# Where the sums of the second layer's weights are made, and how they are stored: a change to a fused attention and token-mixing kernel

## The chip, the cores and the metric

The kernel runs on one core of one Trainium2 chip, as one launch. The time of a run is the device time of that core in microseconds. Before the change the median of three runs is 777.65 us (777.59 to 778.68). The engines that matter here are PE (TensorE, matrix products), DVE (VectorE), ACT (ScalarE), POOL (GpSimd) and SP (SyncE); SP issues most of the DMAs, and ACT issues one kind of load beside its own work. Each of the two has one DMA queue.

## The reference

The first half is an attention over learned memory slots, for 8 batches, 8 heads, 576 positions, 64 channels and 32 slots; the second half is a mixer with a product over the positions and a two-layer product over the 512 channels with 1536 hidden ones:

```
a = exp(phi - max_s(phi)); a = a / sum_s(a)
k_m = a^T k;  v_m = a^T v                    # 32 x 64 for each batch and head
attn = softmax(q k_m^T / sqrt(64));  x = attn v_m      # heads side by side: 576 x 512
h = relu(x^T w_tok1) w_tok2                  # 576 -> 256 -> 576, over the positions
u = x + h^T
out = u + relu(u w_ch1) w_ch2                # 512 -> 1536 -> 512, over the channels
```

All of it is in float32. The kernel splits most values into a high and a low part in the format fp32r, and adds the products high by high, high by low and low by high.

## The kernel before, in words

**Work.** The rows of the mixer, 8 batches by 576 positions, are cut into 9 chunks of 512 rows. The two-layer product of a chunk is the bulk of PE's work. Attention runs beside it, in *quads* (one batch, four of its heads): while PE works on chunk *c*, quads whose rows are needed two or so chunks later go through it step by step. The lines `u`, `Ap`, `Rp`, `sp` of the profile are steps of the quads: `sp` (L766) are the scores, `S` (L773 to L797) the softmax on DVE, `nat` (L136, L137) the split of the attention's output that comes back from DRAM, `Ap` (L908) the first product of the token mixer with it, `Rp` (L927) the hidden part of that mixer, and `u` (L948) its second product.

**Three kinds of chunk.** Chunks 0 to 2 multiply plainly (`cp` L175 and `acc` L198). In chunks 3 to 6, the Quarters, the first layer is done with seven products in place of eight, from sums of quarters of the weights and of quarters of `x` (`qa` and `qb`, L336). Chunks 7 and 8 go together as the Double chunk, where the second layer is done so as well (`da`, `db` L401, `e` and `end` L456). The sums of weights are made once in the kernel, by two classes. `Sums(p)`, p from 0 to 5, makes those of the first layer in chunks 1 and 2 (words, four sums, a split into high and low, a store to DRAM, the rest stored straight from the weights). `Sums2(p)`, p from 0 to 5, does the same for the second layer, where a *pair* p is two of the twelve tiles of 128 hidden channels. Its sums are not read before the Double chunk. From chunk 3 on, PE works from *units*, 512 KB each, which ACT's queue loads back from DRAM (L592 for the first layer, L588 for the second), three units ahead (`AHEAD`).

**Rooms.** Tiles come from rings of rooms under a tag. The tag `c1` has twelve rooms of 4 KB in each partition. They hold the first layer's weights until chunk 3, and then the units (four alive), one tile `whole` and the parts of `x` (five in a chunk). The tag `wide` has five rooms of 8 KB; there are the `uh` and `ul` of the plain chunks, the residual `o`, the temporaries and parts of `x` of the Quarters, and the four sums of a `Sums` or a `Sums2`. A tile in a room waits until all that read or wrote the room's tile before it is done; the ring hands out rooms in the order of the program.

**Order.** The program is written out by a table of events: `at(h, f)` calls `f` when the chunks' main loop reaches the point *h*. A chunk has 24 points, so chunk *c* begins at 24*c*; in the Quarters four points make up one of the six pairs of hidden tiles. Every engine does its instructions in the order in which this table writes them, and so do the two DMA queues' issuers: an instruction that waits holds everything behind it on its engine. Here p = 0 and p = 1 of `Sums2` stand at points 44.5 and 49, at the end of chunk 1 and the beginning of chunk 2; p = 2 to 4 stand 1.5 points after the beginning of chunks 3 to 5, and p = 5 stands 5 points after that of chunk 6. Each has its steps at half-points: two `words` (L488, DVE), four `sum` (L505, DVE), `high` (L509, ACT) and `low` (L513, DVE) for each half, one `store` of 1 MB (L518, SP), and ten points after its start `store_rest` (L525, six DMAs of 128 KB on SP).

**Neighbours on SP's queue.** A quad's softmaxed scores go to DRAM and come back transposed: `rows<-S` (L863, four DMAs of 72 KB), and then `raw<-rows` (L870, L873), which the casts `nat` read. Behind them stand the memory's keys (`keys`, `kb`), `kv`, `q` and `phi` of later quads and the outputs (`out_dram<-o`, L219).

The functions that the change touches, and the lines that call them:

Of the kernel before, what the change touches and what calls it, by code (L numbers as in the profile page):

```python
# [10 lines left out]
F32 = mybir.dt.float32  # L11
F32R = mybir.dt.float32r
# [3 lines left out]
ALU = mybir.AluOpType  # L16
# [4 lines left out]
P = 128  # L21
# [7 lines left out]
def kernel(  # L29
# [25 lines left out]
    nc = tc.nc  # L55
# [8 lines left out]
    DM = w_ch2.shape[3] // 2  # L64
    TT = w_tok1.shape[2] // 2
    NF = 2 * w_ch2.shape[0]
# [9 lines left out]
    WIN, AHEAD = 3, 3  # L76
# [22 lines left out]
    sb = Rooms()  # L99
# [26 lines left out]
    c1 = {}  # L126
    c2h, c2l = {}, {}

    def f32(t):
        return t.bitcast(F32)  # L130
# [16 lines left out]
    def wide(dtype, name):  # L147

        return sb.tile([P, NKK, CW], dtype, tag="wide", name=name, bufs=5)


    class Chunk:
# [24 lines left out]
        def high(s, ps, f):  # L177
            h = sb.tile([P, CW], F32R, tag="hh", name=f"hh{f}" + s.n, bufs=2)
            l = sb.tile([P, CW], F32R, tag="hl", name=f"hl{f}" + s.n, bufs=2)
            s.hid[f] = (h, l)  # L180
            relu_high(h, ps)

        def low(s, ps, f):
            relu_low(*s.hid[f], ps)
# [33 lines left out]
        def store(s, w=slice(0, CW), channels=slice(0, NKK), eng=nc.sync):  # L218
            eng.dma_start(out=out[s.c, :, channels, w], in_=s.o[:, channels, w])  # L219
# [248 lines left out]
    class Sums2:  # L468


        to = dram.tile([P, 7, NF // 4, 1024], F32, name="sums2", tag="sums2", bufs=1)
# [4 lines left out]
        def at(s, i, n=1):  # L476
            w = slice(s.p % 2 * 512, s.p % 2 * 512 + 512)
            return s.to[:, i : i + n, s.p // 2, w]

        def words(s, j):  # L480
            h, l = (t[s.p][:, j] for t in (c2h, c2l))
            if not j:
                if s.p < 2:
                    s.w = [sb.tile([P, DM], F32, tag="al", name=f"v{j}{s.p}", bufs=2) for j in range(2)]
                else:
                    t = sb.tile([P, 2, DM], F32, tag="c1", name=f"v{s.p}", bufs=NF)
                    s.w = [t[:, j] for j in range(2)]
            nc.vector.tensor_tensor(out=s.w[j], in0=f32(h), in1=f32(l), op=ALU.add)  # L488

        def sum(s, o):  # L490
            if o == 1:
                t = wide(F32R, f"sums2{s.p}").rearrange("p a n -> p (a n)")
                s.t = t.rearrange("p (o y) -> p o y", o=4)
                s.v = t.rearrange("p (o x m) -> p o x m", o=4, x=2)

            def at(o):
                return f32(s.v[:, o, 1])

            (w11, w21), (w12, w22) = ((w[:, : DM // 2], w[:, DM // 2 :]) for w in s.w)
            if o == 1:  # L500
                x, y, op = w21, w22, ALU.add
            else:
                x, y = {0: (at(1), w11), 2: (w11, w21), 3: (w12, at(0))}[o]
                op = ALU.subtract
            nc.vector.tensor_tensor(out=at(o), in0=x, in1=y, op=op)  # L505

        def high(s, y):
            v = s.v[:, 2 * y : 2 * y + 2]
            nc.scalar.copy(out=v[:, :, 0], in_=f32(v[:, :, 1]))  # L509

        def low(s, y):
            v = s.v[:, 2 * y : 2 * y + 2]
            nc.vector.tensor_tensor(  # L513
                out=v[:, :, 1], in0=f32(v[:, :, 1]), in1=f32(v[:, :, 0]), op=ALU.subtract
            )

        def store(s):
            nc.sync.dma_start(out=s.at(2, 4), in_=f32(s.t))  # L518

        def store_rest(s):  # L520
            h, l = (t[s.p] for t in (c2h, c2l))
# [457 lines left out]
    class Piece:  # L979
# [9 lines left out]
        def __init__(s, *parts):  # L989
            s.parts, s.words = parts, sum(part.words for part in parts)  # L990
# [79 lines left out]

    class PartW2:
        words, loads, move = NT * HALF, 1, 1.6

        def __init__(s, hf):
# [14 lines left out]
    class PartC1:  # L1089


        words, loads, move = 2 * DM, 1, 2.75

        def __init__(s, f):
# [16 lines left out]

    class PartC2:
        words, loads, move = DM, 0.5, 1.375
        held = []

# [49 lines left out]
    def step(eng, us, fn, *after, take=(), use=(), move=0.0, port=False, other=None):  # L1165
        steps.append(Step(eng, us, fn, after, list(take), list(use), move, port, other))
        return steps[-1]
# [641 lines left out]
    def piece(tags, *parts, after=(), more=()):  # L1809
# [3 lines left out]
        raw = Room(*tags)  # L1813
        z = step(
            "SP", 0.5 * sum(part.loads for part in parts), lambda: p.load(raw), *after,
            take=[raw, *more], move=sum(part.move for part in parts),
        )
        loads.append(z)
# [31 lines left out]
    a, c = quads[0, 0], quads[0, 1]  # L1850
# [94 lines left out]
    z = second.plan_phi()  # L1945
    step("SP", 0.5, second.load_kv, take=[kv2], move=3.5)
    step("SP", 0.5, second.load_q, quads[1, 1].x_s, take=[q2], move=1.6)
    o0, y = Room(("wide", 5)), products[-4]
    for x in range(NKK):
        y = step(  # L1950
            "POOL", 1.4, lambda x=x: chunks[0].residual([x]), *a.lows, *c.lows, y,
            use=[*room0] + ([o0] if x else []), take=[] if x else [o0],
        )
# [30 lines left out]
    while starts[-1][:2] != (B - 1, 1):  # L1984
        b, Q, m, r = starts[-1]
        starts.append((b + Q, 1 - Q, r + 5, r + NF))
    for b, Q, m, r in starts:
        qd = second if b == 2 and not Q else Quad(b, Q)
        fine = b > 2
        if qd is not second:  # L1990
            at(max(m - (16 if b > 4 else 11), 2 * NF), qd.load_phi)
            if fine:
                w = 1.5 * ((b, Q) == (5, 0))
# [46 lines left out]
    for c in range(2, DOUBLE + 1):  # L2040
        h = 2 * NF * (c - 1)
# [18 lines left out]
    for c in range(DOUBLE):  # L2060
        h = 2 * NF * (c + 1)
# [13 lines left out]
    for n in range(AHEAD):  # L2075
        at(2 * NF * WIN - 4 + n, load_unit, n, k=1)
    for p in range(NF // 2):
        x, h = Sums2(p), 2 * NF * (WIN + p - 2) + (1.5 if p < 5 else 5) if p > 1 else 44.5 + 4.5 * p
        at(h + 10, x.store_rest, k=1)
        for y, (fn, *z) in enumerate(  # L2080
            ((x.words, 0), (x.words, 1), (x.sum, 1), (x.sum, 0), (x.sum, 3), (x.sum, 2),
             (x.high, 0), (x.low, 0), (x.high, 1), (x.low, 1), (x.store,))
        ):
            at(h + y / 2, fn, *z, k=1)
    double, h = Double(DOUBLE), 2 * NF * DOUBLE
    at(h - 12, double.mix, "T1", "12", "11", ALU.subtract, k=1)
    at(h - 11, double.high, "11", k=1)
# [20 lines left out]
    for g in range(NF, NF * WIN):  # L2108
        c, f = g // NF, g % NF
        high, low = chunks[c].ch1(f)  # L2110
        run(2 * g - 1, 1)
        run(2 * g - 0.5, -1, 0, 1)
        high()
        low()
        run(2 * g, 0)
        before[0].ch2(before[1])
        run(2 * g, 1)
        run(2 * g + 0.5, -1, 0, 1)
        run(2 * g + 1, -1, 0)
        before = (chunks[c], f)  # L2120
# [91 lines left out]
    for p in range(NF // 2):  # L2212
        h, n = 2 * NF * DOUBLE + 4 * p, n0 + 4 * p
        pool, tag = ((pat, "at"), (pch, "ch"))[p % 2]
# [3 lines left out]
        def bank_(x):  # L2218
            return pool.tile([P, CW], F32, tag=tag, name=f"d{x}{p}", bufs=2)
# [9 lines left out]
        a = bank_("a")  # L2229
# [37 lines left out]
    def gather(t, m, ps, store):  # L2267
        for a in range(2):
            o = oc[t].o[:, 2 * m + a]
            nc.vector.tensor_tensor(out=o, in0=ps[a], in1=o, op=ALU.add)  # L2270
        if store:
            oc[t].store(channels=slice(2 * m, 2 * m + 2))
# [4 lines left out]
    for i, name in enumerate(double.order[:-1]):  # L2277
        y = name in ("21", "T1", "22")
        for p in range(NF // 2):
            k = i * (NF // 2) + p  # L2280
# [20 lines left out]
    for x, (a, w, pool, tag, n) in enumerate(last):  # L2301
# [8 lines left out]
        o = oc[0].o[:, 2 + a, w]  # L2310
# [85 lines left out]
```

## Time and profile before

| | |
|---|---|
| median of 3 runs | 777.65 us (777.59 to 778.68) |
| the profiled execution | 775.13 us |
| its span (first to last instruction) | 773.3 us |
| TensorE's mean granted clock in it | 0.985 of full speed |
| PE busy | 748.2 us, 97% of the span |
| DVE, ACT, POOL busy | 516.7, 342.5, 105.1 us |
| HBM | 121.57 MB read, 35.91 MB written |

The profiled execution is one run under the profiler; its span lies 1.8 us below its own time, and its own time 2.5 us below the median of the runs. A row of the waits says which engine's line waited for which engine's line, with the sum of such idle times in us, their number and the longest. In a row of a timeline stand the start, the busy time, the engine, the line, the operation, the tile written and the tiles read; in brackets the time that the engine was idle before it and what ended that. A row of windows gives for a stretch of the span the busy time and the number of instructions of PE, PE's weight loads, DVE, ACT and POOL, and then the clock that was granted to PE, the busy share of the DMA engines and GB/s. For a DMA a timeline shows only its issue; the time until it has landed stands in the rows of the DMA issues.

### The profile page before, as it was taken

What the parts mean: (1) busy time and instruction counts of PE and PEld (TensorE: products, weight loads), DVE (VectorE), ACT (ScalarE), POOL (GpSimd) and SP (SyncE); (2) the same over time, 40 slices, a digit from 0 to 9 for tenths busy, and PEclk for the clock granted to TensorE, in tenths of its full rate; (3) what the DMA queues carried; (4) which work ended last, traced back from release to release, by engine and by line L of the source; (5) the groups of instructions that cost most, each with busy time, mean ns of one, the idle gap of its engine ahead of it and who ended that gap; (6) DMA issues with size and microseconds to landing.
All of it is one profiled execution on the core that took longest, in us unless ns stands there. A gap on an engine that the chain in (4) does not pass through costs nothing.

```text
span 773.3 us, 12829 instructions
## 1 busy us (share of the span) xinstructions
PE 748.2 (97%) x4883; PEld 639.9 (83%) x4883; DVE 516.7 (67%) x920; ACT 342.5 (44%) x740; POOL 105.1 (14%) x90
## 2 busy tenths in 40 slices
PE   9999999999998899998999899998999999999998
PEld 8777788787876688787898798987898998888886
DVE  4989874687577576874487647874585645544874
ACT  5897653242313333444363534544363544234530
POOL 2143343011302020111010101020010100000000
PEclk9999999999999799999999999999999999999999
DMA  8954631674816644869486875778475944666655
GB/s 345 415 199 157 223 102 29 172 227 134 286 17 218 231 133 151 263 206 316 140 250 238 243 264 155 269 211 306 140 211 183 279 140 152 220 192 201 217 167 189
DMA packets 98366, 158.34 MB, mean 205 GB/s; under 512 B 42112, under 2 KB 65536, under 8 KB 94208
## 3 DMA queue, kind: packets, MB, share of 16 engines
q1 hardware_dynamic: 77712, 91.05, 35.1%
q10 hardware_dynamic: 20592, 66.46, 27.6%
q8 instruction: 39, 0.64, 0.3%
q14 instruction: 23, 0.19, 0.1%
HBM read 121.57 MB, written 35.91 MB: 204 GB/s over the span
## 4 chain that ended last, share of the span: by engine, by line
PE 74%; DVE 10%; DMA 8%; ACT 3%; issue 2%; SPq 1%; POOL 1%; ACTq 0%; DVEq 0%; POOLq 0%
PE acc L198 24%; PE cp L175 8%; PE qa L336 8%; PE u L948 7%; PE qb L336 6%; PE e L456 4%; PE da L401 4%; DMA sums<-sums 3%; PE db L401 3%; PE Ap L908 3%; PE u L1610 2%; PE sp L766 1%; PE Rp L927 1%; DMA raww<-in_w_tok_dram 1%; DMA raw<-rows 1%
## 5 line engine op out<-in xcount | busy, mean ns | idle before, releaser
L198 PE MATMUL acc<-qhh,c 128*128 128x512 f32 x256 | 101.2, 401 | 0.0
L198 PE MATMUL acc<-hh,c 128*128 128x512 f32 x288 | 99.5, 405 | 0.0
L336 PEld LDWEIGHTS qb<-x,unit 128*128 128x128 f32 x432 | 62.6, 194 | 17.0 <-ACT whole L2144 11.0
L336 PE MATMUL qb<-x,unit 128*128 128x256 f32 x432 | 65.1, 288 | 9.7 <-ACT whole L2144 9.7
L336 PEld LDWEIGHTS qa<-xT,unit 128*128 128x128 f32 x432 | 62.2, 192 | 7.8 <-ACT whole L2144 1.3
L198 PEld LDWEIGHTS acc<-hh,c 128*128 128x128 f32 x288 | 55.9, 194 | 15.2 <-issue 3.2
L336 PE MATMUL qa<-xT,unit 128*128 128x256 f32 x432 | 63.7, 284 | 0.9 <-ACT whole L2144 0.9
L2147 DVE TENSOR_TENSOR whole<-whole 128x256 f32<-128x256 f32 x48 | 25.4, 528 | 56.4 <-ACT whole L2144 56.0
L198 PE MATMUL acc<-hl,c 128*128 128x512 f32 x144 | 58.0, 403 | 0.6 <-DVE hl L143 0.6
L839 POOL TENSOR_TENSOR a<-aT,a 64x576 fp32r<-64x576 f32 x22 | 34.0, 1544 | 180.0 <-ACT a L838 157.2
L198 PEld LDWEIGHTS acc<-qhh,c 128*128 128x128 f32 x256 | 49.0, 192 | 9.4 <-issue 3.3
L198 PE MATMUL acc<-qal,c 128*128 128x512 f32 x192 | 54.7, 394 | 0.0
L198 PE MATMUL acc<-qhl,c 128*128 128x512 f32 x128 | 51.4, 402 | 0.0
L175 PE MATMUL cp<-uh,c1h 128*128 128x512 f32 x144 | 51.4, 397 | 0.0
L175 PE MATMUL cp<-ul,c1h 128*128 128x512 f32 x144 | 50.3, 390 | 0.0
L175 PE MATMUL cp<-uh,c1l 128*128 128x512 f32 x144 | 50.3, 390 | 0.0
L143 DVE SCALAR_TENSOR_TENSOR hl<-cp,hh 128x512 fp32r<-128x512 f32 x36 | 24.7, 685 | 35.4 <-ACT hh L140 35.2
L2144 ACT COPY whole<-qa 128x256 f32<-128x256 f32 x72 | 26.7, 371 | 43.0 <-PE qa L336 40.1
L948 PE MATMUL u<-w2h,Rh 128*128 128x288 f32 x112 | 33.5, 299 | 3.3 <-ACT Rh L140 3.3
L198 PEld LDWEIGHTS acc<-qal,c 128*128 128x128 f32 x192 | 32.3, 189 | 3.0
L948 PE MATMUL u<-w2h,Rl 128*128 128x288 f32 x112 | 33.5, 299 | 0.7 <-DVE Rl L143 0.7
L140 ACT ACTIVATE hh<-cp 128x512 fp32r<-128x512 f32 x36 | 21.5, 597 | 26.8 <-PE cp L175 26.7
(286 smaller groups left out, 1702.7 us busy)
## 6 DMA issues: line engine op xcount, KB each, us to landing
unit<-sums ACTq DMA_DIRECT2D x111, 512.0 KB, 4.0
kv<-in_kv_dram SPq DMA_DIRECT2D x12, 1280.0 KB, 7.1
rawc<-in_w_ch_dram SPq DMA_DIRECT2D x12, 1024.0 KB, 10.4
q<-in_q_dram SPq DMA_DIRECT2D x16, 576.0 KB, 6.2
unit<-sums ACTq DMA_DIRECT2D x30, 256.0 KB, 3.6
sums<-sums SPq DMA_DIRECT2D x12, 512.0 KB, 5.7
sums<-sums SPq DMA_DIRECT2D x6, 1024.0 KB, 6.5
phi<-in_phi_dram SPq DMA_DIRECT2D x16, 320.0 KB, 4.2
```

The costliest lines, as they stand in the source:

```text
L140: nc.scalar.activation(out=h, in_=ps, func=AF.Relu)
L143: nc.vector.scalar_tensor_tensor(out=l, in0=ps, scalar=0.0, in1=f32(h), op0=ALU.max, op1=ALU.subtract)
L175: nc.tensor.matmul(ps, l[:, a, w], r[:, a], start=n == 0, stop=n == len(mm) - 1)
L198: nc.tensor.matmul(ps, l_[f // 2][:, f % 2, a * P : (a + 1) * P], r[:, w], start=f == start and x == 0, stop=f == end - 1 and x == 2,)
L336: nc.tensor.matmul(ps[:, :HW], l, r, start=first and n == 0, stop=n == len(mm) - 1, skip_group_check=not first,)
L401: nc.tensor.matmul(ps, l, r, start=first and n == 0, stop=n == len(mm) - 1, skip_group_check=not first,)
L456: nc.tensor.matmul(ps, weights[:, x, m], r[:, w], start=first and n == 0, stop=last and n == 2, skip_group_check=name in ("T2", "T3", "22"),)
L839: s.low_eng.tensor_tensor(out=l, in0=s.aT[own], in1=f32(h), op=ALU.subtract)
L908: nc.tensor.matmul(ps[:, :TT], a, w, start=x == 0, stop=x == len(mm) - 1)
L948: nc.tensor.matmul(ps[:, :HALF], a, r, start=x == 0, stop=x == len(mm) - 1)
L2144: nc.scalar.copy(out=to, in_=ps[:, :HW])
L2147: nc.vector.tensor_tensor(out=to, in0=x, in1=y, op=ALU.add)
```

## The change

`Sums2` gets two tiles of the tag `c1`, one for each half of its four sums, and makes everything inside them: the words in the high places, the sums in the low places, then the high parts over the words, then the low parts over the sums. Before, the words were in tiles of the tag `al` (p = 0, 1) or in one `c1` tile (p = 2 to 5), and the sums in a `wide` tile. The operations on DVE and ACT are the same in number and size. The store is cut into two of 512 KB, one for each half; the first follows three points after the pair's start, the second, with its `low`, 5.5 points after.

The pairs move: p = 0 to 3 stand 3.5 points after the beginning of chunks 3 to 6, p = 4 and p = 5 in the Double chunk, 1.5 and 9.5 points after its beginning. `store_rest` stands at point 84 + 12p, so from the middle of chunk 3 to the beginning of chunk 6.

```diff
         def words(s, m):
+            if m:
+                s.v = [
+                    sb.tile([P, 2, 2, DM // 2], F32R, tag="c1", name=f"v{y}{s.p}", bufs=NF)
+                    for y in range(2)
+                ]
+            h, l = (f32(t[s.p][:, :, m * DM // 2 : (m + 1) * DM // 2]) for t in (c2h, c2l))
+            nc.vector.tensor_tensor(out=f32(s.v[1 - m][:, :, 0]), in0=h, in1=l, op=ALU.add)
...
-        def store(s):
-            nc.sync.dma_start(out=s.at(2, 4), in_=f32(s.t))
+        def store(s, y):
+            t = s.v[y].rearrange("p o x m -> p o (x m)")
+            nc.sync.dma_start(out=s.at(2 + 2 * y, 2), in_=f32(t))
...
-        x, h = Sums2(p), 2 * NF * (WIN + p - 2) + (1.5 if p < 5 else 5) if p > 1 else 44.5 + 4.5 * p
-        at(h + 10, x.store_rest, k=1)
-        for y, (fn, *z) in enumerate(
-            ((x.words, 0), (x.words, 1), (x.sum, 1), (x.sum, 0), (x.sum, 3), (x.sum, 2),
-             (x.high, 0), (x.low, 0), (x.high, 1), (x.low, 1), (x.store,))
+        x, h = Sums2(p), 2 * NF * (WIN + min(p, 4)) + (3.5, 1.5, 9.5)[max(p - 3, 0)]
+        at(2 * NF * WIN + 12 + 12 * p, x.store_rest, k=1)
+        for y, fn, *z in (
+            (0, x.words, 1), (0.5, x.words, 0), (0.5, x.sum, 1), (1, x.sum, 0), (1, x.sum, 2),
+            (1.5, x.sum, 3), (2, x.high, 0), (2.5, x.high, 1), (3, x.low, 0), (3, x.store, 0),
+            (5.5, x.low, 1), (5.5, x.store, 1),
         ):
-            at(h + y / 2, fn, *z, k=1)
+            at(h + y, fn, *z, k=1)
```

The order on two engines shows what moves. The number at the end of a name counts tiles through the program and differs between the two kernels; line numbers above 480 are eleven smaller in the changed kernel. The first place is DVE at the end of chunk 1, from the reduction of a quad's `phi` to the softmax `S` of another quad. Before, with `v` and `sums` of pair 0 of `Sums2`:

```order
L621 TENSOR_REDUCE pr_1_2146<-phi_1_1900 128x128
L505 TENSOR_TENSOR sums_2150<-v_2128,v_2129 128x256
L143 SCALAR_TENSOR_TENSOR hl_1_2153<-cp_1_2132,hh_1_2152 128x512
L230 TENSOR_TENSOR ul_1668<-u_2_1_2156,uh_1667 128x288
L230 TENSOR_TENSOR ul_1668<-u_2_1_2167,uh_1667 128x96
L773 STREAM_TRANSPOSE S_0_2189<-sp_3_0_2179 128x288
L773 STREAM_TRANSPOSE S_0_2189<-sp_3_0_2180 128x288
L505 TENSOR_TENSOR sums_2150<-sums_2150,v_2128 128x256
L780 TENSOR_REDUCE mx_0_2205<-S_0_2189 128x18
L505 TENSOR_TENSOR sums_2150<-v_2129,sums_2150 128x256
```

The same place of the changed kernel:

```order
L610 TENSOR_REDUCE pr_1_2142<-phi_1_1900 128x128
L143 SCALAR_TENSOR_TENSOR hl_1_2147<-cp_1_2129,hh_1_2146 128x512
L230 TENSOR_TENSOR ul_1668<-u_2_1_2150,uh_1667 128x288
L230 TENSOR_TENSOR ul_1668<-u_2_1_2161,uh_1667 128x96
L762 STREAM_TRANSPOSE S_0_2183<-sp_3_0_2173 128x288
L762 STREAM_TRANSPOSE S_0_2183<-sp_3_0_2174 128x288
L769 TENSOR_REDUCE mx_0_2198<-S_0_2183 128x18
```

The sums of pair 0 no longer stand in front of `hl` and `ul`, nor between the steps of the softmax.

The second place is SP's queue in chunk 3. There `rows`, `raw`, `keys` and `kb` belong to a quad, `kv` to a later one, and `sums_101` is the DRAM tile that all of `Sums2` writes. Before:

```order
L863 DMA rows_1_3439<-S_1_3335 32x18x32 x4
L518 DMA sums_101<-sums_3245 128x4x512
L870 DMA raw_1_3492<-rows_1_3439 128x4x128
L873 DMA raw_1_3492<-rows_1_3439 64x128
L719 DMA keys_0_3500<-T_0_3497 32x2x32 x4
L612 DMA kv_1_3538<-in_kv_dram 128x2560
L728 DMA kb_0_3587<-keys_0_3500 64x128 x2
```

The same place of the changed kernel, where `v_3234` and `v_3235` are the two halves of pair 0:

```order
L852 DMA rows_1_3397<-S_1_3291 32x18x32 x4
L507 DMA sums_101<-v_3234 128x2x512
L859 DMA raw_1_3451<-rows_1_3397 128x4x128
L862 DMA raw_1_3451<-rows_1_3397 64x128
L708 DMA keys_0_3459<-T_0_3456 32x2x32 x4
L601 DMA kv_1_3497<-in_kv_dram 128x2560
L507 DMA sums_101<-v_3235 128x2x512
L717 DMA kb_0_3548<-keys_0_3459 64x128 x2
```

Between `rows` and `raw` stands half a store in place of a whole one, and the other half stands behind `kv`, in front of `kb`. Chunks 4 and 5 have the same order. In chunk 6 the store of before stood behind `raw`, and now the first half stands in front of it there as well:

```order
L863 DMA rows_1_6376<-S_1_6293 32x18x32 x4
L870 DMA raw_1_6423<-rows_1_6376 128x4x128
L873 DMA raw_1_6423<-rows_1_6376 64x128
L518 DMA sums_101<-sums_6361 128x4x512
L525 DMA sums_101<-c_1242 128x256 x6
```

The changed kernel in chunk 6:

```order
L852 DMA rows_1_6362<-S_1_6277 32x18x32 x4
L507 DMA sums_101<-v_6236 128x2x512
L859 DMA raw_1_6408<-rows_1_6362 128x4x128
L862 DMA raw_1_6408<-rows_1_6362 64x128
L507 DMA sums_101<-v_6237 128x2x512
```

The six DMAs of `store_rest` that followed there now stand in front of this piece, at the beginning of the chunk.

## Rows read from the trace of the kernel before

**Rows 1.** The page's first part: busy time of each engine.

```profile
PE 748.2 (97%) x4883; PEld 639.9 (83%) x4883; DVE 516.7 (67%) x920; ACT 342.5 (44%) x740; POOL 105.1 (14%) x90
```

**Rows 2.** Waits of PE: line, releaser, us in total, times, longest.

```profile
PE qb L336 <- ACT whole L2144: 9.7, 3, 3.5
PE u L948 <- ACT Rh L140: 3.3, 1, 3.3
PE sp L766 <- DVE ul L230: 1.7, 1, 1.7
...
PE Ap L908 <- DVE nat L137: 1.4, 2, 1.2
...
PE acc L198 <- DVE hl L143: 0.6, 1, 0.6
```

**Rows 3.** Waits of DVE, the two for a room.

```profile
DVE sums L560 <- DMA out_dram<-o: 4.9, 1, 4.9
...
DVE sums L505 <- POOL o L210: 2.4, 1, 2.4
```

**Rows 4.** Waits of ACT, the one for a DMA of `sums`.

```profile
ACT x L285 <- DMA sums<-sums: 8.8, 3, 3.4
```

**Rows 5.** Windows of 20 us: early chunks, chunk 3, chunk 6, Double chunk.

```profile
200.00:220.00 20.00, 18.30 (x100) 15.12 (x99) 11.41 (x20) 5.25 (x12) 6.98 (x5) 0.91 0.52 165
240.00:260.00 20.00, 15.54 (x76) 11.11 (x75) 13.85 (x25) 5.71 (x12) 2.26 (x2) 0.82 0.86 317
340.00:360.00 20.00, 16.61 (x96) 14.68 (x95) 13.26 (x28) 9.05 (x23) 2.85 (x2) 0.91 0.85 262
580.00:600.00 20.00, 20.00 (x140) 17.48 (x139) 12.02 (x26) 7.05 (x20) 0.00 (x0) 1.00 0.55 183
660.00:680.00 20.00, 20.00 (x90) 16.58 (x89) 9.75 (x15) 6.79 (x12) 0.00 (x0) 1.00 0.60 207
```

**Rows 6.** Timeline of ACT at 212 us, the last cast ahead of `ul`.

```profile
212.03 0.24 ACT L227 CAST uh<-u 128x96 fp32r<-128x96 f32 x1
```

**Rows 7.** Timeline of DVE at 212 us, behind its wait.

```profile
212.03 0.42 DVE L505 TENSOR_TENSOR sums<-v,v 128x256 f32<-128x256 f32 x1 [2.42 <-POOL o L210]
...
212.97 0.61 DVE L230 TENSOR_TENSOR ul<-u,uh 128x288 fp32r<-128x288 f32 x2
```

**Rows 8.** Timeline of SP's issues: an output's store, chunk 3, chunk 6.

```profile
242.66 0.43 SPq L219 DMA_DIRECT2D out_dram<-o  x1
...
344.39 3.17 SPq L863 DMA_DIRECT2D rows<-S  x4
347.66 0.45 SPq L518 DMA_DIRECT2D sums<-sums  x1
351.69 0.38 SPq L870 DMA_DIRECT2D raw<-rows  x1
...
600.11 2.37 SPq L863 DMA_DIRECT2D rows<-S  x4
604.70 0.38 SPq L870 DMA_DIRECT2D raw<-rows  x1
```

**Rows 9.** DMA issues of 340 to 372 us: KB each, us to landing.

```profile
raw<-rows SPq DMA_DIRECT2D x1, 256.0 KB, 3.4
```

**Rows 10.** DMA issues of the whole span: KB each, median us to landing.

```profile
unit<-sums ACTq DMA_DIRECT2D x111, 512.0 KB, 4.0
...
sums<-sums SPq DMA_DIRECT2D x12, 512.0 KB, 5.7
sums<-sums SPq DMA_DIRECT2D x6, 1024.0 KB, 6.5
```

**Rows 11.** Timeline of DVE in chunk 6, the low part of `nat`.

```profile
608.80 0.69 DVE L137 TENSOR_TENSOR nat<-raw,nat 128x512 fp32r<-128x512 f32 x1 [0.22 <-ACT nat L136]
```

**Rows 12.** Timeline of PE in chunk 6, the first product with `nat`.

```profile
610.31 0.28 PE L908 MATMUL Ap<-w1h,nat 128*128 128x256 f32 x1
```

**Rows 13.** Timeline of ACT's queue in chunk 6, a load of a unit.

```profile
612.18 0.33 ACTq L592 DMA_DIRECT2D unit<-sums  x1
```

More of the change, by code (lines that the diff above doesn't have):

```diff
@@ L478, in at @@
             return s.to[:, i : i + n, s.p // 2, w]
[L480 to L488, printed above, removed]
@@ L490, in sum, with words @@
-        def sum(s, o):
[L491 to L505, printed above, removed]
+        def words(s, m):
+            if m:
[5 more added lines that the diff above has]
+            nc.vector.tensor_tensor(out=f32(s.v[1 - m][:, :, 0]), in0=h, in1=l, op=ALU.add)
@@ L507, in high @@
+        def sum(s, o):
+            w21, w22, w11, w12 = (f32(v[:, f, 0]) for v in s.v for f in range(2))
+            s0, s1, s2, s3 = to = [f32(v[:, f, 1]) for v in s.v for f in range(2)]
+            x, y, op = (
+                (s1, w11, ALU.subtract), (w21, w22, ALU.add),
+                (w11, w21, ALU.subtract), (w12, s0, ALU.subtract),
+            )[o]
+            nc.vector.tensor_tensor(out=to[o], in0=x, in1=y, op=op)
         def high(s, y):
-            v = s.v[:, 2 * y : 2 * y + 2]
@@ L509, in high @@
-            nc.scalar.copy(out=v[:, :, 0], in_=f32(v[:, :, 1]))
+            nc.scalar.copy(out=s.v[y][:, :, 0], in_=f32(s.v[y][:, :, 1]))
         def low(s, y):
[L512 to L515, printed above, removed]
-        def store(s):
-            nc.sync.dma_start(out=s.at(2, 4), in_=f32(s.t))
+            h, l = (s.v[y][:, :, x] for x in range(2))
+            nc.vector.tensor_tensor(out=l, in0=f32(l), in1=f32(h), op=ALU.subtract)
```

## The prediction

> **What bounds the kernel now.** I read the busy times first. PE works 748.2 us of a span of 773.3 [rows 1], so about 25 us of PE's time are idle, and nothing that shortens another engine's work counts unless it ends one of these gaps. The second view is the waits of PE, which splits the gaps by what ended them [rows 2]. Most of what is to be seen there is not the start of the kernel but a few stops in its middle: three of `qb` for `whole` on ACT, one of `u` for `Rh`, one of `sp` for `ul`, two of `Ap` and one of `acc`. The third view is the waits of the engines that PE waited for. DVE stood 4.9 us in front of a first-layer sum until a store of an output had landed, and 2.4 us in front of a second-layer sum until POOL had finished a residual [rows 3]; ACT stood three times in front of a part of `x`, 8.8 us in all, until a store of sums had landed [rows 4]. All three are waits for a room under the tag `wide`: the instruction that opens a tile waits for the room's last user. The fourth view is the clock in windows. Where PE has stood, the granted clock of that stretch is 0.82 to 0.91; where it has not, it is 1.00 [rows 5]. So each such stop costs twice, once as idle time and once as a stretch at the lower level (1.2 in place of 2.4 GHz).
>
> **The change part by part.** The sums go against the profiled execution, 775.13 us, which lies 2.5 us below the median of the runs; I add that at the end.
>
> *Pairs 0 and 1 leave chunks 1 and 2.* The first `wide` tile of pair 0 is what DVE waited for until 212.03 [rows 3, 7]. Behind that wait stood `hl` and `ul`, and PE waited 1.7 us for `ul` to begin the scores [rows 2]. Without it `ul` is held only by ACT's cast, which ends at 212.03 + 0.24 = 212.27 [rows 6], in place of 212.97 [rows 7]; the second of the two `ul` ends with it some 0.31 later, at 212.6 in place of 213.6. That saves 1.0. The wait of `acc` for `hl` (0.6) and the longer one of `Ap` for `nat` (1.2, of which I take 1.0) stand in chunk 2 among pair 1's words and sums [rows 2]: two words of 0.69 by the size of [rows 11] and four sums of 0.42 [rows 7], 3.1 us of DVE before the lows, more than either wait. They go: 1.6.
>
> *The ring of `wide` turns two places less in chunk 2.* There the first-layer sum of pair 4 got the room of an output whose store had been issued at 242.66 [rows 8]; DVE waited 4.9 us for its landing [rows 3], `Rl` and what follows came late, and PE stood 3.3 us in front of `u` [rows 2]. Two fewer tiles ahead of it give that sum a room that has long been read. I save 3.3. The room of the stored output goes to a later tile of ACT's, the fourth `u` of the quads, which may wait a little for the same landing: between 0 and the whole 3.3; it stands later than the sum did, so I take 0.5.
>
> *Pairs 2 to 5 take no `wide` room in the Quarters.* The wait of ACT's `x` for the store of 1 MB [rows 4] has nothing left to wait for, and PE's three stops of `qb`, 9.7 us [rows 2], go with it. What is late next? In chunk 6 the pair stood later, no part of `x` met its store, and PE was busy for the whole of 20 us at clock 1.00 [rows 5]; so the same work without this wait has no gap behind it.
>
> *The clock.* A window's loss is (1 − clock) × 20 us: 1.8 for 200 to 220, 3.6 for 240 to 260, 1.8 for 340 to 360 [rows 5] and the same for the corresponding stops of chunks 4 and 5, 10.8 together. From the mean clock of the execution, 0.985, all of it is 0.015 × 773.3 = 11.6. I take 11.0.
>
> *Two `c1` rooms for each pair.* Twelve rooms less four units, `whole` and five parts of `x` leave two, and the pair takes just these, from its words to the landing of its stores. What takes the room next is a load of a unit, issued on ACT's queue, three units ahead of use. In chunk 6 such a load is issued at 612.18, that is 12.1 us after that chunk's `rows` (600.11) [rows 8, 13]. The first half's store is issued where the whole one was, 3.3 us after `rows` [rows 8], and 512 KB of this kind land after 5.7 [rows 10]: 9.0, so 3 us to spare. The second half's room is wanted three units later. I price it at 0; it can't gain, since no load waits there now, and its upper end is the slower rival's price.
>
> *Half a store between `rows` and `raw`.* In chunk 3 `raw` was issued at 351.69 and landed 3.4 later [rows 8, 9], 10.7 us after `rows` at 344.39. In chunk 6, where no store stood in front, the same steps give 604.70 + 3.4 − 600.11 = 8.0. So a whole store costs `raw` 2.7 us. There `nat` ended at 609.49 [rows 11] and PE began `Ap` at 610.31 [rows 12] without having waited: 0.8 us to spare. Half of the 2.7 less 0.8 is 0.55 for each of four chunks, 2.2 us. The ends are 0 (nothing, if PE reaches `Ap` later) and (2.7 − 0.8) × 4 = 7.6, if half a store holds `raw` as long as a whole one. I take the 2.2 because the wait of `raw` is for bytes in front of it.
>
> A rule speaks against that halving. On an engine of the DMA, the Trainium skill says ("DMA: Bandwidth & Descriptors", section Queues, rings and completion order), descriptors are consumed in ring order, so `raw` stands behind all of the half store; the trace agrees in that `raw` came 2.7 us later behind a store. The same page (Anatomy of one DMA) fits a transfer, for another issue path, as 2.0 us fixed and bytes at 436 GB/s; the rows have 5.7 for 512 KB and 6.5 for 1 MB, so here too most of the time does not shrink with the size. By the page's byte part alone, 1.2 us (an estimate), `raw` would come 0.4 late, and the sum would be 0.6 us lower.
>
> *The pairs' work on DVE and ACT* is the same in count, and DVE is busy 9.75 of 20 us in the Double chunk, where two pairs go [rows 5]. 3.1 us of DVE for a pair, plus lows, spread over six points, hide beside PE's products; if that cover fails, a pair costs up to the 1.0 that pair 1 cost `Ap`. I take 0. The six `store_rest` stand alone and nothing waits for them until the Double chunk: 0.
>
> The sum: waits 1.0 + 1.6 + 3.3 + 9.7 = 15.6, clock 11.0, together 26.6 saved; 0.5 + 2.2 = 2.7 new; net 23.9. 775.13 − 23.9 = 751.2 profiled, and 2.5 more is 753.7 us as a median of runs.
>
> **The rivals.**
>
> *Nothing new waits.* Slack in `Ap` covers the half store and ACT's `u` comes free: 753.7 − 2.7 = 751.0. For it: PE in chunk 6 reached `Ap` only 0.8 behind, but with PE's gaps gone each quad's chain may come earlier by as much. Against: PE too comes earlier.
>
> *Half a store holds `raw` like a whole one.* 7.6 in place of 2.2 is 759.1; if each stop of 1.9 us also brings the low clock for part of its window, up to 1.8 × 4 = 7.2 more, 766. For it: 512 KB take 5.7 against 6.5 [rows 10]. I put it at 760.
>
> *The early stops pass on.* When `sp` and `u` no longer wait, the next late thing in chunk 2 does, since DVE is busy 13.85 of 20 us there [rows 5] and the stored output's room still has a user behind it. Then the 3.3 of `u` and its 3.6 of clock stay: 760.6.
>
> *Unit loads are held (the slower one).* If a half lands more than 12.1 us after `rows`, ACT stands at the unit load, everything behind it on ACT (casts, `relu`) stands too, and PE stops in front of `whole` as it did in chunk 3. A price from there is 9.7 / 3 = 3.2 of wait and 1.8 of clock, 5.0 each. Eight halves in chunks 3 to 6 would make 40: 794; it is slower than before from five of eight on. For it: both spare rooms are taken, and the second half is issued only behind `kv`. Against: the 3 us of margin, and units that land in 4.0 [rows 10].
>
> **How the numbers follow.** My forecast has 0.55, nothing new 0.12, the full price at `raw` 0.18, the early stops 0.10, the held loads 0.05, of which about 0.04 reaches past 777.65. A difference of 0.2%, 1.6 us, is what a measurement of this kernel can tell from none. All other cases end over 10 us below before, so faster has 0.93; I leave 0.03 for a mix of held loads and kept gains within 0.2%, and 0.04 for slower. The forecast's own range is 749.5 to 758 (clock 10 to 12, `raw` 0 to 1.4 each). The range reaches from below the case where nothing waits, 748, to the full price at `raw` with most of its clock, 765; it leaves out the held loads and half of the tails.
>
> **What would show it.** Right: the list of ACT's waits has no `x` behind `sums`, DVE's none of a `sums` for a store or POOL; PE's has no `qb` behind `whole` over 1 us in chunks 3 to 5, and the windows there grant 1.00. A wait of `Ap` for `nat` of about half a us in chunks 3 to 6 would show the half store's price; one near 2 us the full one. Wrong: unit loads on ACT that wait for `sums`, with gaps of `qa` or `qb` after them, or in chunk 2 a `u` that still waits 3 us.

## The result, and the profile after

The changed kernel takes 751.33 us (751.25 to 755.71, four runs) against 777.65 us before (777.59 to 778.68, three runs; a fourth, of 1467.88, lies far outside and is left out). The ratio is 0.9671, with a 95% interval from 0.9627 to 0.9715: faster, by 26.3 us of medians. The forecast was 753.7, its range 748 to 765. The profiled execution took 751.26 us, where the working had 751.2.

The page's first part, busy times of the engines after the change:

```profile
PE 738.3 (99%) x4883; PEld 631.4 (84%) x4883; DVE 514.5 (69%) x920; ACT 343.5 (46%) x740; POOL 104.7 (14%) x90
```

Beside [rows 1] PE's busy time is 9.9 us shorter with the same 4883 instructions, which is put down to the clock, and the span went from 773.3 to 749.5, so PE's idle time from 25.1 to 11.2, which is 13.9 less. The forecast had 11.0 for the clock and 15.6 − 2.7 = 12.9 for the waits.

The waits of PE after the change (line, releaser, us in total, times, longest):

```profile
PE pp L1278 <- POOL mask L105: 1.6, 1, 1.6
PE end L456 <- DMA unit<-sums: 1.3, 1, 1.3
PE at L1553 <- ACT raww L1015: 0.9, 1, 0.9
PE qb L336 <- ACT whole L2134: 0.9, 2, 0.4
PE qa L336 <- ACT whole L2134: 0.7, 1, 0.7
PE Ap L897 <- DVE nat L137: 0.7, 3, 0.3
...
PE u L937 <- DVE Rl L143: 0.3, 1, 0.3
PE sp L755 <- DVE ul L230: 0.2, 1, 0.2
```

Beside [rows 2]: `qb` from 9.7 to 0.9, `u` for `Rh` and `acc` for `hl` gone, `sp` from 1.7 to 0.2, `Ap` from 1.4 to 0.7. Two rows went the other way: `end` waits 1.3 for a unit in the Double chunk, where it waited 0.4, and `at`, a product at the start of the kernel, has a wait of 0.9 that before does not show. (Line numbers from the table of events on are ten smaller than before, not eleven: `whole` is L2144 there and L2134 here.) The waits that [rows 3] and [rows 4] show are not among the new kernel's: no `sums` of DVE waits for a store or for POOL, and no `x` of ACT for a store.

The same windows as in [rows 5] (after the stretch: PE, its weight loads, DVE, ACT and POOL, then the clock, the DMA share and GB/s):

```profile
200.00:220.00 20.00, 19.78 (x111) 16.18 (x110) 8.51 (x15) 5.43 (x13) 6.47 (x5) 1.00 0.53 171
240.00:260.00 20.00, 20.00 (x143) 16.33 (x145) 13.14 (x23) 6.26 (x14) 1.95 (x2) 1.00 0.66 260
...
340.00:360.00 20.00, 19.77 (x133) 18.00 (x132) 11.09 (x22) 8.84 (x24) 1.81 (x2) 1.00 0.91 323
...
580.00:600.00 20.00, 20.00 (x137) 18.57 (x136) 10.37 (x19) 9.61 (x26) 1.11 (x1) 1.00 0.61 203
...
660.00:680.00 20.00, 20.00 (x90) 16.54 (x89) 10.48 (x16) 8.09 (x15) 0.00 (x0) 1.00 0.75 248
```

All of these stretches are at 1.00, the upper level, and the mean clock of the execution is 1.000.

SP's issues in chunks 3 and 6, to be held against [rows 8]:

```profile
330.19 2.26 SPq L852 DMA_DIRECT2D rows<-S  x4
332.56 0.86 SPq L507 DMA_DIRECT2D sums<-v  x1
336.13 0.38 SPq L859 DMA_DIRECT2D raw<-rows  x1
...
575.38 2.43 SPq L852 DMA_DIRECT2D rows<-S  x4
577.92 0.45 SPq L507 DMA_DIRECT2D sums<-v  x1
580.02 0.38 SPq L859 DMA_DIRECT2D raw<-rows  x1
```

`raw` is issued 5.9 after `rows` in chunk 3 (7.3 before, behind the whole store) and 4.6 in chunk 6 (4.6 before, behind none). The DMA issues of 330 to 350 us and of 575 to 592 us give its time to landing in the last column:

```profile
raw<-rows SPq DMA_DIRECT2D x1, 256.0 KB, 4.4
```

```profile
raw<-rows SPq DMA_DIRECT2D x1, 256.0 KB, 4.0
```

So it is there 10.3 us after `rows` in chunk 3 and 8.6 in chunk 6.

### The profile page after: what moved, and what is told of

The parts are those of the page before. It is cut to its first block, busy times and chain, and to the rows that moved or that the text cites. A ratio compares the mean times of both kernels' runs of the same rounds, so it can differ in the third digit from the quotient of the medians.

```text
span 749.5 us, 12863 instructions
## 1 busy us (share of the span) xinstructions
PE 738.3 (99%) x4883; PEld 631.4 (84%) x4883; DVE 514.5 (69%) x920; ACT 343.5 (46%) x740; POOL 104.7 (14%) x90
## 4 chain that ended last, share of the span: by engine, by line
PE 57%; DVE 8%; DMA 5%; ACT 2%; SPq 1%; issue 1%; POOL 0%; ACTq 0%; DVEq 0%; POOLq 0%
PE acc L198 18%; PE qa L336 7%; PE qb L336 5%; PE u L937 5%; PE e L456 4%; PE da L401 4%; PE db L401 3%; PE cp L175 3%; PE Ap L897 2%; DMA rows<-S 1%; DMA raw<-rows 1%; PE sp L755 1%; PE sp L656 1%; PE end L456 1%; DMA sums<-c1h 1%; DMA sums<-sums 1%
## 5 line engine op out<-in xcount | busy, mean ns | idle before, releaser
L198 PE MATMUL acc<-hh,c 128*128 128x512 f32 x288 | 96.5, 394 | 0.0
L336 PEld LDWEIGHTS qa<-xT,unit 128*128 128x128 f32 x432 | 60.7, 188 | 8.6 <-ACT whole L2134 2.9
L336 PEld LDWEIGHTS qb<-x,unit 128*128 128x128 f32 x432 | 60.9, 188 | 8.2 <-ACT whole L2134 2.2
L198 PEld LDWEIGHTS acc<-hh,c 128*128 128x128 f32 x288 | 54.1, 188 | 14.1 <-issue 2.7
L336 PE MATMUL qb<-x,unit 128*128 128x256 f32 x432 | 63.2, 282 | 0.9 <-ACT whole L2134 0.9
L198 PE MATMUL acc<-hl,c 128*128 128x512 f32 x144 | 56.2, 390 | 0.0
L2134 ACT COPY whole<-qa 128x256 f32<-128x256 f32 x72 | 26.9, 374 | 53.4 <-PE qa L336 44.9
L2134 ACT COPY whole<-qb 128x256 f32<-128x256 f32 x48 | 17.8, 370 | 33.9 <-PE qb L336 33.7
```

The lines of the kernel that those rows point to most:

```text
L198: nc.tensor.matmul(ps, l_[f // 2][:, f % 2, a * P : (a + 1) * P], r[:, w], start=f == start and x == 0, stop=f == end - 1 and x == 2,)
L336: nc.tensor.matmul(ps[:, :HW], l, r, start=first and n == 0, stop=n == len(mm) - 1, skip_group_check=not first,)
L2134: nc.scalar.copy(out=to, in_=ps[:, :HW])
```

## The experiments

In each the edit is told against the kernel that it starts from. All times are medians. The experiments ran in three groups, each on one chip with the kernel before beside it, which took 777.4 to 778.7. The changed kernel itself ran beside the second group alone (rooms held, stores late, the half store behind `raw` once more) and took 750.66 (749.57 to 751.01); in the first group the comparison is with the 751.33 of the result.

**Both parts of the change apart.** The pairs 0 and 1 go back to chunks 1 and 2, with their old tiles; pairs 2 to 5 are made in c1 rooms, in chunks 3 to 6, each with its `store_rest` ten points after its start (code cut):

```diff
-        x, h = Sums2(p), 2 * NF * (WIN + min(p, 4)) + (3.5, 1.5, 9.5)[max(p - 3, 0)]
+        if p < 2:
+            x, h = Sums2Whole(p), 44.5 + 4.5 * p
...
+        x, h = Sums2(p), 2 * NF * (WIN + p - 2) + 3.5
```

> Pairs 0 and 1 of the second layer's sums stay at the end of chunk 1 and in chunk 2 as before (al and wide tiles); pairs 2 to 5 are made in two c1 rooms each, 3.5 points into chunks 3 to 6, stores by halves. Theory (both parts of the gain stand apart): the early part is worth 1.0 + 1.6 + 3.3 of waits and 1.8 + 3.6 of clock, less 0.5, so 10.8 us: 751.3 + 10.8 = 762, with PE's stop of 1.7 in front of sp, of 3.3 in front of u and windows at 0.91 and 0.82 between 200 and 260 us, and no stop of qb in chunks 3 to 5. Rival (the early stops only hide others, as in the prediction's rival): the early part is worth 4 or less: 755 or less.

Measured: 761.05 us (759.88 to 761.31), ratio to before 0.9764 (0.9733 to 0.9794). PE's first waits and DVE's wait for the store:

```profile
PE u L978 <- ACT Rh L140: 3.1, 1, 3.1
PE Ap L938 <- DVE nat L137: 1.9, 4, 1.2
PE sp L796 <- DVE ul L230: 1.6, 1, 1.6
```

```profile
DVE sums L590 <- DMA out_dram<-o: 4.7, 1, 4.7
```

The early part is worth 761.05 − 751.33 = 9.7, or 10.05 between the profiled executions, where 10.8 was forecast. The stops of the early stretch were not standing in front of others: they come back nearly as they were when only the early pairs come back, `acc` for `hl` (0.6) and the longer one of `Ap` (1.2) too. The clock came back in part. The window behind `u` is at 0.83, near the 0.82 that was forecast, but the one with the stop of `sp` is not at 0.91:

```profile
200.00:220.00 20.00, 18.43 (x108) 15.41 (x107) 12.32 (x20) 5.29 (x13) 7.24 (x5) 1.00 0.51 163
```

Where chunk 3 begins, with PE's first product `qa`, shows the early part alone. First the changed kernel, then this one:

```profile
302.22 0.88 PE L336 MATMUL qa<-x,unit 128*128 128x256 f32 x6
```

```profile
311.82 0.88 PE L336 MATMUL qa<-x,unit 128*128 128x256 f32 x6
```

That is 9.6 us. The kernel before began chunk 3 at 314.72, so 12.5 later than the changed one: its windows of 200 to 220 and 260 to 280 us were at 0.91 and 0.92, and here both are at 1.00. So the later pairs are worth 13.8 of the profiled 23.9 by this experiment, and 11.4 by the two traces.

One stop is new here: `Ap` waits 1.2 for `nat` on ACT, in chunk 6. There half a store stands in front of `raw`, which lands 10.8 us after `rows`. More of this below.

**The ring without the pairs' work.** Two wide tiles are opened in the changed kernel where the pairs opened theirs:

```diff
+    def turn(p):
+        t = wide(F32, f"turn{p}")
+        h, l = (f32(x[p][:, 0, : DM // 2]) for x in (c2h, c2l))
+        nc.vector.tensor_tensor(out=t[:, 0, : DM // 2], in0=h, in1=l, op=ALU.add)
+
+    for p in range(2):
+        at(45.5 + 4.5 * p, turn, p, k=1)
```

> The changed kernel with two more wide tiles opened at the points where pairs 0 and 1 opened theirs before, each written by one addition of 128x256 on DVE and read by nobody: two turns of the ring without the pairs' work. Theory (the rooms cost, not the work): DVE waits 2.4 in front of the first tile for POOL's residual and 4.9 in front of pair 4's first-layer sum for an output's store; PE stops 1.7 at sp and 3.3 at u, with the low clock behind both: 1.0 + 3.3 + 1.8 + 3.6 = 9.7 more, 761. Rival (the pairs' work in DVE's line made it late): two additions of 0.4 cost under 1: 752.

Measured: 751.16 us (748.71 to 756.79), near what the rival had. DVE's timeline, though, shows the first of the two waits and not the second:

```profile
211.82 0.43 DVE L2079 TENSOR_TENSOR turn<-c 128x256 f32<-128x256 f32 x1 [3.05 <-POOL o L210]
...
240.62 0.41 DVE L549 TENSOR_TENSOR sums<-w,w 128x256 f32<-128x256 f32 x1
```

The second row is pair 4's first-layer sum, which waits for nothing here. The first wait cost little: PE stopped 0.9 in front of `sp`, and chunk 3 began 0.9 later than in the changed kernel. That the second wait is missing fits a tile that is only written and so is free again at once, so that the sum need not take the output's room. The prediction had spoken of a ring that turns. For the second wait the theory had not been tested yet: the tile must be *held*.

**The rooms held.** The same two tiles, written a second time four points later, so that each keeps its room for some 18 us:

```diff
+    for p in range(2):
+        at(45.5 + 4.5 * p, hold, p, 0, k=1)
+        at(49.5 + 4.5 * p, hold, p, 1, k=1)
```

> The changed kernel with two more wide tiles, each opened where pairs 0 and 1 opened theirs before and kept until four points later (two additions of 128x256 on DVE each, nobody reads them), so that pair 4's first-layer sum gets the room of the output whose store is under way, as before; the pairs' own work stays in chunks 3 to 7. Theory (the room is what made DVE stand and PE stop): DVE waits 3 to 5 us for the store's landing and about 3 for POOL's residual; PE stops about 3 at u, with the low clock behind it (3.6), and under 1 at sp: 757 to 758. Rival (the waits stop PE only on top of the pairs' work in DVE's line): under 2 us more, 751 to 753.

Measured: 760.39 us (758.45 to 761.74), so 9.7 more than the changed kernel on the same chip. PE's waits:

```profile
PE u L937 <- ACT Rh L140: 4.8, 1, 4.8
PE Ap L897 <- ACT nat L136: 2.0, 1, 2.0
...
PE sp L755 <- DVE ul L230: 1.2, 1, 1.2
```

DVE's two waits in its timeline:

```profile
210.99 0.42 DVE L2082 TENSOR_TENSOR held<-c 128x256 f32<-128x256 f32 x1 [3.35 <-POOL o L210]
...
246.34 0.43 DVE L549 TENSOR_TENSOR sums<-w,w 128x256 f32<-128x256 f32 x1 [6.46 <-DMA out_dram<-o]
```

The windows:

```profile
200.00:220.00 20.00, 18.77 (x109) 15.72 (x108) 8.18 (x16) 4.94 (x11) 6.11 (x5) 1.00 0.50 157
...
240.00:260.00 20.00, 15.14 (x68) 10.80 (x67) 9.87 (x17) 3.84 (x7) 1.64 (x2) 0.74 0.68 259
```

Four additions of 0.4 us, and most of the loss of the early part is back. Chunk 3 begins 8.8 us later than in the changed kernel, where it was 9.6 with the pairs themselves:

```profile
311.04 0.88 PE L336 MATMUL qa<-x,unit 128*128 128x256 f32 x6
```

So for the stops of `sp` and `u` it was the room that cost the time and not the pairs' work. The stops of `acc` and `Ap` in chunk 2 are the other way round: they came back with the pairs and do not come back here, so they belong to the pairs' work in DVE's line. The 9.7 of the median is therefore no second measurement of the same sum. A part of it lies in chunk 6, where `Ap` waits the 2.0 of the list for `nat`, behind a `raw` that lands 11.5 us after `rows`, and the clock falls:

```profile
580.00:600.00 20.00, 17.82 (x104) 15.68 (x103) 12.03 (x23) 8.41 (x22) 2.93 (x2) 0.91 0.76 227
```

Both kernels, the one with the rooms held and the one that turns, open the same tiles in the same order, and only one of them makes the sum wait. So rooms are not handed out in strict turn, and where a tile goes depends on when the others come free; the rule itself is not shown by these runs.

The stop of `u` is even longer than before (4.8 against 3.3): DVE asks for the room at 246.34 − 6.46 = 239.9, 4.7 us earlier than before, and the store has landed only 3.1 earlier. The window behind it loses 0.26 × 20 = 5.2 us to the clock, by the prediction's way of counting. The stop of `sp` (1.2) left its window at 1.00.

**When the store lands, alone.** Two kernels take before, and change one number: the point at which pairs 2 to 4 stand in their chunks. The tiles are the same; the pairs' work on DVE and ACT moves along with the store. That the next chunk's `x` still takes the sums' room is seen in the later one, where it waits for it. Earlier, the store stands in front of `rows` on SP:

```diff
-        x, h = Sums2(p), 2 * NF * (WIN + p - 2) + (1.5 if p < 5 else 5) if p > 1 else 44.5 + 4.5 * p
+        x, h = Sums2(p), 2 * NF * (WIN + p - 2) + (0.5 if p < 5 else 5) if p > 1 else 44.5 + 4.5 * p
```

> The kernel before with one number changed: pairs 2 to 4 stand 0.5 points into chunks 3 to 5 in place of 1.5, so that their store of 1 MB stands in front of rows on SP and not behind it; rooms and tiles are the same, and x of the next chunk still takes the sums' wide room. Theory (x waits for the store's landing and for nothing else): the store is issued some 7 us earlier and has landed when x wants the room; ACT's three waits for sums and PE's three stops of qb (9.7) go, and 1.8 of clock with each: 15 us less, 762 to 764. Rival (the pair's work beside x on DVE and ACT, or the room being handed from sums to x at all, is what stops PE): 774 to 778.

Measured: 766.75 us (765.87 to 768.09) beside before's 777.41, ratio 0.9859 (0.9824 to 0.9895). PE's longest waits:

```profile
PE u L948 <- ACT Rh L140: 4.7, 1, 4.7
PE Ap L908 <- ACT nat L136: 3.0, 2, 1.7
PE u L948 <- DVE Rl L143: 1.9, 2, 1.7
PE Ap L908 <- DVE nat L137: 1.8, 4, 1.2
```

The stops of `qb` are gone from the list, and so is `x` from ACT's: the theory's step holds. Of the 15 forecast 10.7 came. With the store in front of `rows`, `raw` is issued 7.1 and 7.2 us after `rows` in chunks 4 and 5 (6.3 and 4.2 before), and `Ap` waits 3.0 there for `nat` on ACT, where before showed no such wait. That gives back a part, `u` for `Rl` another (1.9 against 0.7), and the early `u` a third (4.7 against 3.3); why that one grew was not tried.

Later, with 3.5 in the same place, as in the changed kernel, the store stands behind `raw` and `keys`:

```diff
-        x, h = Sums2(p), 2 * NF * (WIN + p - 2) + (1.5 if p < 5 else 5) if p > 1 else 44.5 + 4.5 * p
+        x, h = Sums2(p), 2 * NF * (WIN + p - 2) + (3.5 if p < 5 else 5) if p > 1 else 44.5 + 4.5 * p
```

> The kernel before with the same number the other way: pairs 2 to 4 stand 3.5 points into their chunks, as the pairs of the changed kernel do, but still with a wide tile and one store, which now stands behind raw and keys on SP. Theory: the store is issued some 6 us later, x waits for its landing about 10 us in place of 3, and PE stops that much longer in three chunks: 3 x 6.6 = 20 us more and more of the low clock, 795 to 805. Rival (what counts is that nothing stands between rows and raw): 765 to 778.

Measured: 787.57 us (785.24 to 792.12), ratio 1.0128 (1.0082 to 1.0175). PE's and ACT's rows for the room:

```profile
PE qb L336 <- ACT whole L2144: 23.2, 3, 8.4
```

```profile
ACT x L285 <- DMA sums<-sums: 21.2, 3, 7.8
```

The store at the changed kernel's point, but with a wide room, costs 10 us more than before instead of 26 less. So that point gained nothing by itself; that the sums no longer hold a wide room did. The forecast price was too high twice: `x` waited 7.8 at the longest and not 10, and the clock hardly added to it. PE's stops of `qb` are 13.5 us longer than before, and PE's busy time, 749.4, is only 1.2 above before's.

**What stands in front of raw.** Both halves at once, as the whole store before, but in c1 rooms:

```diff
-            (5.5, x.low, 1), (5.5, x.store, 1),
+            (3, x.low, 1), (3, x.store, 1),
```

> The changed kernel with the second half's low and store at the first half's point, so that 1 MB stands between rows and raw in chunks 3 to 6. Theory A (the bytes in front of raw hold it, 2.7 us for 1 MB): raw lands 10.7 after rows in each of these chunks, PE waits for nat about 1.9 in place of 0 to 0.3, four times, some 7 us: 758, and more if the clock falls. Theory B (PE has more slack in front of Ap than the 0.8 read from chunk 6, and raw is held by less): under 2 us, 751 to 753.

Measured: 757.33 us (755.07 to 758.21). PE's waits, longest sums first:

```profile
PE qb L336 <- ACT whole L2134: 1.8, 3, 0.6
...
PE Ap L897 <- DVE nat L137: 1.1, 5, 0.2
PE qa L336 <- ACT whole L2134: 1.1, 1, 1.1
PE Ap L897 <- ACT nat L136: 1.0, 1, 1.0
```

The size is nearer to theory A, 6 us more, but not by its place: `Ap` waits 2.1 us for `nat` in all, 1.4 more than in the changed kernel, and not 7. Longer stops of `qb` and `qa` make up another 1.3. The profiled execution has 3.8 us more span, of which 2.3 are PE's busy time (740.6) at a clock of 1.00; neither this nor the 6 of the median is explained. In chunk 4 `raw` is held by more than theory A says. ACT's timeline there, and SP's:

```profile
424.84 0.62 ACT L136 CAST nat<-raw 128x512 fp32r<-128x512 f32 x1 [2.01 <-DMA raw<-rows]
```

```profile
412.84 2.61 SPq L852 DMA_DIRECT2D rows<-S  x4
415.55 1.00 SPq L507 DMA_DIRECT2D sums<-v  x2
418.77 0.36 SPq L859 DMA_DIRECT2D raw<-rows  x1
```

`raw` landed 6.0 us after its issue, by the DMA issues of this stretch:

```profile
raw<-rows SPq DMA_DIRECT2D x1, 256.0 KB, 6.0
```

That is 11.9 us after `rows`. In the changed kernel's chunk 4, with half a store in front, it took 3.4 from its issue.

The other way, the first half moves behind `raw` and `keys`:

```diff
-            (1.5, x.sum, 3), (2, x.high, 0), (2.5, x.high, 1), (3, x.low, 0), (3, x.store, 0),
+            (1.5, x.sum, 3), (2, x.high, 0), (2.5, x.high, 1), (3, x.low, 0), (4.5, x.store, 0),
```

> The changed kernel with the first half's store 1.5 points later, behind raw and keys and in front of kv. Theory: raw lands 8.0 after rows in all four chunks, the wait of Ap for nat in chunk 3 (0.23) goes, nothing else moves: 751.0. Rival (the rooms come free too late): the half is issued some 5 us later and lands past the 12 us after rows at which a unit load wants its room; ACT stands at that load in some of the four chunks and PE stops in front of whole: 753 to 760.

> The first half's store behind raw and keys once more, beside the changed kernel on the same chip. Theory: it saves the 0.2 to 0.5 us that Ap waits for nat, 0.3 to 1.5 us below the changed kernel's time. Rival: no difference that can be measured.

> The changed kernel itself on this chip: 751.3, within 1.6; its profiled run and its median within 1 us of each other, where before's lie 2.5 to 4 apart.

Measured: 749.81 (749.23 to 752.14) at first, 749.62 (748.44 to 752.95) beside the changed kernel's 750.66 on the same chip. The ranges lie over each other, so no difference can be told, and the first theory's step is too small to be seen in a time: `Ap`'s waits for `nat` on DVE are 0.5 in two places, without the one in chunk 3. `raw` landed 8.4, 8.1, 8.9 and 8.1 us after `rows` in chunks 3 to 6 with no store in front, and 9.0, 9.1, 9.3 and 8.0 the second time, where 8.0 was forecast. The changed kernel's profiled execution in this group took 751.01, 0.35 above its median, as expected within 1 us.

**Stores late.** Both halves move far back, to test the slower rival:

```diff
-            (1.5, x.sum, 3), (2, x.high, 0), (2.5, x.high, 1), (3, x.low, 0), (3, x.store, 0),
-            (5.5, x.low, 1), (5.5, x.store, 1),
+            (1.5, x.sum, 3), (2, x.high, 0), (2.5, x.high, 1), (3, x.low, 0), (7, x.store, 0),
+            (5.5, x.low, 1), (9, x.store, 1),
```

> The changed kernel with the two half stores at 7 and 9 points after the pair's start in place of 3 and 5.5. Theory of the slower rival (a half that lands more than 12.1 us after rows holds a unit load on ACT, which stops PE in front of whole): the first half is issued about 13 us after rows, lands about 19 after, so in each of chunks 3 to 6 ACT stands some 5 to 7 us at the load and PE stops 3 or more with the low clock behind: 4 x 5 = 20 us or more, 771 to 790. Rival (three units ahead cover such a delay): 751 to 755.

Measured: 749.94 us (747.77 to 752.34). ACT's only row for these stores, and PE's largest in the Quarters:

```profile
ACT whole L2134 <- DMA sums<-v: 2.2, 2, 1.7
```

```profile
PE qb L336 <- ACT whole L2134: 0.8, 2, 0.4
```

ACT stood twice for such a store, at most 1.7 us, and PE's stops did not grow. In chunk 3 the load that stood is this one:

```profile
350.56 0.33 ACTq L581 DMA_DIRECT2D unit<-sums  x1
```

`rows` was issued at 328.52 and the first half at 341.46; it landed 9.1 later, which is when the load goes out, 22 us after `rows`. The loads in front of it did not wait for the room. That takes the rival's premise away, that the load which wants the room stands at 12.1 us after `rows` whatever the store does. Which load takes the room in the changed kernel its trace does not show, since none waits.

## Why the prediction was right

**The bound and the three rooms: right.** All three waits for a wide room are gone, with the stops behind them. The two early ones came back when the rooms were held without the pairs' work. The late one, in chunks 3 to 5, went when its store was moved forward in the kernel before, and grew when it was moved back.

**Pairs 0 and 1: right in the main, 10.05 for 10.8.** The wait of `sp` fell by 1.5, not 1.0. The waits of `acc` and `Ap` in chunk 2 are gone, and they were the pairs' work, as forecast. The reason given for the stop of `u` was loose: it isn't that the ring turns less often, but that a room is free when the sum asks for one.

**The clock: near, 9.9 for 11.0.** Count and kind of PE's instructions are unchanged. The sum was near, but that each such stop costs twice does not hold: with the early pairs alone the stop of `sp` left its window at 1.00.

**Half a store in front of raw: mis-sized, in PE's slack.** The prediction had `raw` 1.35 us late and four stops of 0.55, 2.2 in all. The four landings are 10.3, 8.5, 10.0 and 8.6 after `rows`, with a mean of 9.35, which is just 8.0 + 1.35. That agreement is partly luck: with no store in front the same chunks had 8.4 in the mean, and 8.8 in the second execution, so half a store cost 0.5 to 1.0, and from chunk to chunk between 0.2 and 2.0. And in chunks 3 to 6 one wait of `Ap` for `nat` is left, of 0.2. The 0.8 to spare was read at one place of before, chunk 6; in chunks 3 and 5 a `raw` two microseconds later than 8.0 stopped PE by 0.2 at most. The price is there all the same: with `raw` at 10.8 and 11.5 in chunk 6, in the kernel with the early pairs and in the one with the rooms held, `Ap` waited 1.2 and 2.0. Why `raw` came that late there was not tried.

**What was not foreseen.** `end` waits 0.9 longer in the Double chunk, which takes up about half of the 2 us that the half store did not cost. The row is 1.3 and 1.0 in two executions of the changed kernel, and 0.2 to 0.8 in the kernels that differ by a store's place; what sets it was not tried. The 0.9 of `at` is missing in the second execution. The 0.5 set aside for a later `u` of ACT's was not needed: no such wait is in the list.

**Luck in the sum.** The working's 751.2 for the profiled execution met 751.26, but not because each term did. The idle time fell by 13.9 where 12.9 was forecast, and the clock gave 9.9 where 11.0 was forecast; the two misses cancel.

**The term that missed: "2.5 more is 753.7 us as a median of runs".** The whole miss of 2.4 is this offset. It was the place of one execution among the runs of before, which go from 774.63 to 781.71 us in the experiments, and no property of the kernel to be carried over. In the kernels of the experiments the median lies between 1.4 below and 2.3 above the profiled execution, and 0.1 above and 0.35 below it in the changed kernel's two sets. What spreads the runs is not shown. The mean clock alone does not do it, since before's runs at 0.985 go from 774.63 to 780.35. Nor do the long stops alone: the kernel with the turned ring lacks those of `u` and `qb`, and goes from 748.71 to 756.79 at 0.998 to 1.000.

**The range of its own.** 749.5 to 758 is not quite what its terms give: clock 12, `raw` 0 and no wait of `u` make 750.0.

**The rivals.** That nothing new waits (751.0) came nearest to the median, but with the 2.5 in it; without that it stands at 748.5, where the forecast's 751.2 is nearer to the profiled 751.26. Of what it says, that `Ap`'s slack covers the half store is right for this kernel. The full price at `raw` and the passed-on stops didn't happen. The held unit loads didn't, and the experiment with the stores late shows that their premise was wrong.

## What to carry to other kernels

A wait in front of an instruction that opens a tile can be a wait for a room and not for data. Ask who held it and when that landed, and price the stop of the bound engine together with the clock in the window behind it; here the clock was two fifths of the gain. To test such a cause, hold the room and leave out the work, and see in the trace whether the wait came back, and where else the time went, before believing the time. An offset between one execution and the median of runs is no term of a forecast.

## What the runs showed of the hardware

The granted clock does not follow the length of a stop alone. The stop of `sp` was 1.7 us with a window at 0.91 before, and 1.6 us with 1.00 in the kernel that keeps the early pairs. The stop of `u` was 3.3 us with 0.82 before, 4.8 with 0.74 where the rooms are held, and 4.7 with 0.85 in the kernel whose store stands in front of `rows`:

```profile
240.00:260.00 20.00, 14.55 (x72) 10.61 (x73) 12.47 (x22) 4.32 (x9) 1.87 (x2) 0.85 0.90 333
```

So a price of clock read at one stop need not hold for the next. Five windows together gave 10.8 where 9.9 was measured, but 13.5 us more of stops, in the kernel with the later store, took only 1.2 us more of PE's busy time.
